# An FFT convolution with an MLP on one core: reordered loads and transform front, fixed PSUM places, and product PSUM in two pools

## The chip, the cores and the metric

The kernel runs on one core of a Trainium2 chip. The metric is the device time of one execution in microseconds. Besides the time there is a profile of one execution: a page of shares and groups of instructions, and a trace that can be asked for a chain of waits, a timeline, or busy times in stretches. PE is TensorE (matmul, with PEld for its weight loads), DVE is VectorE, ACT is ScalarE, POOL is GpSimd, SP is the engine that issues most of the DMAs.

## The reference

Cut to what matters (S = 2048, D = 512, Dff = 1376, all inputs bf16):

```python
def _A_ref(q, k, v, shift_k, ssm_k, ssm_D):
    k_shift = sum over t of k_pad[:, t:t + S, :] * shift_k[:, ks - 1 - t]     # 4 taps, causal
    kv = k_shift * v
    y = irfft(rfft(kv padded to 2S) * rfft(ssm_k padded to 2S))[:, :S, :]     # causal long convolution
    y = y + kv * ssm_D
    return q * y

x = A_q
h = x + _A_ref(_layernorm(x), A_k, A_v, A_shift_k, A_ssm_k, A_ssm_D)
out = h + relu(_layernorm(h) @ B_w1) @ B_w2
```

## The kernel before

The long convolution is a length-4096 transform written as matmuls in two stages over a 64 by 64 split, and only its odd frequencies are used. Everything is emitted in one order by hand (`manual_schedule`), so each engine works through its instructions in the order of the source, and waits only for the tiles it reads or overwrites. A pool of tiles of one tag hands out its buffers in rotation; a new tile waits until all readers of the one before it in its buffer are done, and a new pool waits for the pools that held its space.

The stages, in order of time:

1. **Loads and tables (0 to 9 us).** SP issues `sk` (the filter, 2 MB, L95) and then eight transposing DMAs, kT and vT for four chunks of 512 tokens (L111 to L114). ACT issues `wsh` (L97) and the two `draw` loads of ssm_D (L102), spread over 64 rows each. DVE makes integer phases (`tsn` L189, `tcs` L206), ACT turns them into sine and cosine tables (`table`, L184; `cc_part` makes one of four pieces of the cosine table). POOL makes the diagonal tap weights `wdiag` (L222), the first-stage tables `f1hi`/`f1lo`, the negated sines `c2n` (L229), the block-diagonal tables `f2hi`/`f2lo` (L234) and `dtab`, a copy of `draw` (L235).
2. **Row transposes (9 to 16).** `to_rows` (L246) makes eight PE transposes of 128x128 each into one PSUM tile `pst` and copies it to `kfl`, on DVE and ACT in turn; eight calls.
3. **Taps and first stage of the filter (16 to 41).** Eight groups: `taps(c, h)` (L303) makes two accumulations of four matmuls into the two banks of one tile `pkv`, and DVE multiplies each by v into `sk`'s space (L310); `stage1` (L252) makes 64 small matmuls, each with 32 rows, into two PSUM tiles of two banks, which are copied to `a1k` (L239 on ACT, L241 on DVE). With `pairs` it makes 32 matmuls with 64 rows and the tables f2hi/f2lo instead. Three `cc_part` tables go between the groups on ACT. The PE instructions of a group are 8 tap matmuls and 64 first-stage matmuls, with as many weight loads (the page counts both).
4. **Transposes of kv (41 to 45, L340) and second stage of the filter (45 to 60, `stage2`, L281 and L283)** into `kf`, with dtab added (L363).
5. **First stage of kv (60 to 71)**: eight `stage1` calls with pairs, copied to `a1x`, the first tile of each by ACT, the second by DVE.
6. **Product (71 to 102).** For each of 16 frequency pairs: `product` makes the second stage into `u0`, `u1`, multiplied by kf on DVE and POOL; two steps later `finish` combines the products by matmuls with plus or minus the identity into `psy0`, `psy1` (L408), and copies them back over kf (L239, L241). x (`load_x`, L419) and w1 (L430) are loaded meanwhile.
7. **First inverse stage (102 to 120, `inv1`, L528)**: 16 calls into `psi1` tiles, copied to `ax`. Between the calls stand the layer norm of x, the twiddles `ecore` and the centring of w1: `column_means(n)` (L504) makes the mean of a quarter of w1's columns by matmuls into a tile `pm`; `center` subtracts it, for n = 0 and 1 on DVE out of PSUM, for n = 2 and 3 on POOL after a DVE copy to `wm` (L555).
8. **Second inverse stage, gating, MLP (121 to 218)**: `inv2` (L592) into `psz` and `psz0`, `gate` (L574, L577) on DVE, then `mlp1` (L604) and `mlp2` (L621), with the later `inv2` calls between them.

[...] Stages 2 to 5 share one pool `psF` of four two-bank tiles with one tag: `pst`, `pkv`, `ps1`, `pst2` and `ps2k` all rotate through it. The product stage has `psP`, two buffers each of u0, u1, psy0 and psy1, a bank each. The inverse has `psI` (three two-bank tiles) and `psC` (two one-bank `pm` tiles), both pushed after psP is popped, so that their first tiles wait for all readers of psP.

Of the kernel before, what the change touches and what calls it, by code (L numbers as in the profile page):

```python
# [9 lines left out]
ALU = mybir.AluOpType  # L10
# [46 lines left out]
def kernel(  # L57
# [32 lines left out]
    kvp = pl.push("kvp", side="right")  # L90
    psum = pl.push("psF", bufs=4, space=PSUM)

# [6 lines left out]
    draw = consts.tile([P, DC, 64], BF16, name="draw")  # L99
    for dp in range(2):  # L100
        src = bass.AP(tensor=A_ssm_D.tensor, offset=A_ssm_D.offset + 64 * dp, ap=[[0, 64], [P, DC], [1, 64]])
        nc.scalar.dma_start(out=draw[64 * dp:64 * dp + 64, :, :], in_=src)  # L102
    vT = [vp.tile([P, DC, 512], BF16, name=f"vT{c}") for c in range(4)]
# [5 lines left out]
    for c in range(4):  # L109
        if c == 0:  # L110
            nc.sync.dma_start_transpose(out=kT[c][:, :, 16:CH + 16], in_=k_d[0:CH, :])  # L111
        else:
            nc.sync.dma_start_transpose(out=kT[c][:], in_=k_d[CH * c - 16:CH * c + CH, :])
        nc.sync.dma_start_transpose(out=vT[c][:], in_=v_d[CH * c:CH * c + CH, :])  # L114


# [62 lines left out]
    def wrap(t, M):  # L179
        nc.vector.tensor_single_scalar(out=t, in_=t, scalar=M - 1, op=ALU.bitwise_and)  # L180
# [24 lines left out]
    _sin(dsc[:], t3[:], 64)  # L205
    nc.vector.tensor_single_scalar(out=tcs[:], in_=tsn[:], scalar=2048.0, op=ALU.add)  # L206
    wrap(tcs[:], 8192)
    cc_parts = [(p, dp) for p in cc for dp in range(2)]

    def cc_part():  # L210
        p, dp = cc_parts.pop(0)
        table(p, tcs, dp)
# [12 lines left out]
    nc.gpsimd.tensor_tensor(out=f1f[:], in0=f1f[:], in1=f1hi[:, 0:64], op=ALU.subtract)  # L225
    nc.gpsimd.tensor_copy(out=f1lo[:, 0:64], in_=f1f[:])
    for a, b in ((0, 8), (8, 16), (16, 22), (22, 24), (24, 32)):
# [3 lines left out]
    for f, g in ((f1hi, f2hi), (f1lo, f2lo)):  # L231
        for rg in range(DC):
            rows = slice(32 * rg, 32 * rg + 32)
            nc.gpsimd.tensor_copy(out=g[rows, 64 * (rg % 2):64 * (rg % 2) + 64], in_=f[rows, :])  # L234
    nc.gpsimd.tensor_copy(out=dtab[:], in_=draw[:].rearrange("p r g -> p g r"))  # L235

    def copy(eng, o, i):
        if eng == "A":
            nc.scalar.copy(out=o, in_=i)  # L239
        else:  # L240
            nc.vector.tensor_copy(out=o, in_=i)  # L241

    def bank2(name):
        return psum.tile([P, 2, 512], F32, tag="ps", name=name)

    def to_rows(src, q, fl, eng):  # L246
        pst = psum.tile([P, 2, 8, P], BF16, tag="ps", name="pst")
        for i in range(8):
            nc.tensor.transpose(out=pst[:, 0, i, :], in_=src[:, :, :, 8 * q + i], identity=ident[:])  # L249
        copy(eng, fl[:, :, :, 8 * q:8 * q + 8], pst[:, 0, :, :].rearrange("p i (d g) -> p g d i", d=2))  # L250

    def stage1(fl, a_out, gb, engs, pairs=False):  # L252

        pss = [bank2("ps1") for _ in range(2)]
        n, tabs = (2, (f2hi, f2lo)) if pairs else (4, (f1hi, f1lo))
        K = P // n
        for gi in range(8):
            for f in range(2):
                for t in range(n):
                    rows = slice(K * t, K * t + K)  # L260
                    if pairs:
                        o = pss[t][:, gi // 4, 128 * (gi % 4):128 * (gi % 4) + 128]
                    else:
                        o = pss[t // 2][:, t % 2, 64 * gi:64 * gi + 64]
                    nc.tensor.matmul(out=o, lhsT=fl[rows, 8 * gb + gi, :, :].rearrange("p d n -> p (d n)"),  # L265
                                     rhs=tabs[f][rows, :], start=(f == 0), stop=(f == 1),
                                     tile_position=(K * t, 0), skip_group_check=True)
# [35 lines left out]
    def taps(c, h):  # L303
        ps = bank2("pkv")
        for i in range(2):
            for j in range(KS):
                nc.tensor.matmul(out=ps[:, i, :], lhsT=wdiag[:, 2 * h + i, j, :],  # L307
                                 rhs=kT[c][:, 2 * h + i, 16 - j:CH + 16 - j], start=(j == 0), stop=(j == KS - 1))
        for i in range(2):
            nc.vector.tensor_tensor(out=kvp2[:, :, 2 * h + i, 8 * c:8 * c + 8, :].rearrange("p m a e -> p a m e"),  # L310
                                    in0=ps[:, i, :].rearrange("p (a m e) -> p a m e", a=8, e=2),
                                    in1=vT[c][:, 2 * h + i, :].rearrange("p (a m e) -> p a m e", a=8, e=2),
                                    op=ALU.mult)
# [16 lines left out]
    nc.gpsimd.tensor_copy(out=k1o[:], in_=k1i[:])  # L330
    nc.gpsimd.memset(mhalf[:], -0.5)
    pl.pop("kvp")
    xfp = pl.push("xfp", side="right")
# [3 lines left out]
    for q in range(8):  # L337
        pst = psum.tile([P, 4, P], F32, tag="ps", name="pst2")
        for i in range(4):
# [28 lines left out]
    for gb in range(8):  # L368
        stage1(xfl, a1x, gb, "AD", pairs=True)
    pl.pop("psF")  # L370
# [14 lines left out]
    def product(kp):  # L385
# [3 lines left out]
        for s in range(2):  # L389
            u = psum.tile([P, 2, 256], F32, tag=f"u{s}", name=f"u{s}")  # L390
            stage2(u, a1x, kp, s)
# [11 lines left out]
    def finish(at):  # L403
        kp, (tr, ti) = pending.pop(0)
        for s, (a, b, m) in enumerate(((tr[:, 0], ti[:, 1], ineg), (tr[:, 1], ti[:, 0], ipos))):
            psy = psum.tile([P, 512], F32, tag=f"psy{s}", name=f"psy{s}")
            for m_, t_, first in ((ipos, a, True), (m, b, False)):
# [24 lines left out]
    load_x(2)  # L432
    load_x(3)
    while pending:
        finish(16)
    pl.pop("psP")
    pl.pop("prod")
# [14 lines left out]
    act_pool = {0: late, 1: late}  # L452
    psum = pl.push("psI", bufs=3, space=PSUM)
    psum1 = pl.push("psC", bufs=2, space=PSUM)

# [44 lines left out]

    FS = 344
    cen = {}

    def column_means(n):  # L504
        cen[n] = psum1.tile([P, 512], F32, tag="pm", name="pm")
        for c in range(DC):
            nc.tensor.matmul(out=cen[n][:, 0:FS], lhsT=ones[:], rhs=w1[:, c, n * FS:(n + 1) * FS],
                             start=(c == 0), stop=(c == DC - 1))

    def center(eng, n, mean):  # L510
# [3 lines left out]

    wm = late.tile([P, 2, FS], F32, name="wm")

    ec_turns(0)
    ln1_stats(0)
    ec_turns(1)
    column_means(0)  # L520
    column_means(1)

# [13 lines left out]
    for b in range(16):  # L536
# [73 lines left out]
    def mlp2(sc, hook=None):  # L610
        h1T = h1s[sc]
        for i in range(4):
# [18 lines left out]
            if hook is not None:  # L631
                hook(i)

    pl.pop("psC")
    pl.pop("psI")
    psz = pl.push("psZ", space=PSUM)
# [84 lines left out]
```

## Time and profile before

| | us |
|---|---|
| six runs, median | 219.46 |
| lowest and highest | 217.75, 220.78 |
| the profiled execution, in all | 220.12 |
| its span, first to last instruction | 218.2 |

Busy time of each engine, its share of the span and number of instructions, and the busy tenths of 40 equal slices (5.46 us each) with the granted TensorE clock in tenths:

```profile
PE 195.7 (90%) x2251; PEld 137.9 (63%) x2267; DVE 143.4 (66%) x236; ACT 115.7 (53%) x177; POOL 79.1 (36%) x120
...
PE   0389879899997999998999799999999999999991
...
PEclk9999979999999999999999999999999999999999
```

A digit of 9 is 90% or more. Before 9.3 us PE has no data; from then on it is nearly always busy, and the clock is full but for slice 5 (27.3 to 32.7 us). [...] A wait is shown at the instruction that had to wait, with what released it; "issue" stands for a wait that no semaphore in the profile explains.

### The profile page before, as it was taken

The page shows a single profiled execution, that of the slowest core. Times are in us where ns is not written, and L with a number is a line of the kernel's source. Part 1 is how long each engine was busy: PE and PEld are TensorE (multiplying, and loading weights), DVE is VectorE, ACT ScalarE, POOL GpSimd, SP SyncE. Part 2 cuts the span into 40 slices and gives each one's busy share as a digit, 9 for nine tenths or more (in the row PEclk, how much of TensorE's full clock was granted, in tenths as well). Part 3 has the DMA queues.
Part 4 walks back from the last instruction along what each step waited for, and adds up shares of the span by engine and source line. Part 5 has one row for each costly group of instructions (what it writes and reads, how often), then busy time and mean ns, then how long its engine had stood idle before and what let it go on. Part 6 is the DMA issues. An engine that isn't in the chain of part 4 may idle for free.

```text
span 218.2 us, 5459 instructions
## 1 busy us (share of the span) xinstructions
PE 195.7 (90%) x2251; PEld 137.9 (63%) x2267; DVE 143.4 (66%) x236; ACT 115.7 (53%) x177; POOL 79.1 (36%) x120
## 2 busy tenths in 40 slices
PE   0389879899997999998999799999999999999991
PEld 0385434699986899995999754655646644444451
DVE  7965746776689899998495993897395470243031
ACT  2977718765598588885897138401550046016400
POOL 3299992000001899997648702020202011002000
PEclk9999979999999999999999999999999999999999
DMA  5999950000000004836932789394453430010012
GB/s 197 299 195 219 152 122 3 5 2 3 0 5 3 0 3 112 223 119 178 196 72 37 226 159 171 61 195 88 94 96 65 101 79 3 24 49 24 0 45 56
DMA packets 49513, 20.08 MB, mean 92 GB/s; under 512 B 44400, under 2 KB 47952, under 8 KB 49488
## 3 DMA queue, kind: packets, MB, share of 16 engines
q1 hardware_dynamic: 46816, 18.18, 40.2%
q10 hardware_dynamic: 2672, 1.54, 2.7%
q8 instruction: 18, 0.29, 0.6%
q14 instruction: 7, 0.06, 0.1%
HBM read 7.08 MB, written 2.10 MB: 42 GB/s over the span
## 4 chain that ended last, share of the span: by engine, by line
PE 81%; DVE 9%; DMA 5%; issue 2%; SPq 1%; ACT 1%; DVEq 0%; ACTq 0%
PE ps1m L604 18%; PE ps2m L621 15%; PE pkv L307 7%; PE psi L528 7%; PE psy L408 7%; PE pz L592 5%; DVE a1x L241 4%; DMA sk<-in_A_ssm_k_dram 4%; PE ps2k L281 3%; PE ps2k L283 3%; PE u L281 3%; PE u L283 3%; PE ps L265 3%; PE pst L249 3%; PE pst L340 2%
## 5 line engine op out<-in xcount | busy, mean ns | idle before, releaser
L606 ACT ACTIVATE h1T<-ps1m 128x512 bf16<-128x512 f32 (+1 forms) x44 | 26.0, 596 | 55.4 <-PE ps1m L604 55.4
L621 PE MATMUL ps2m<-w,h1T 128*128 128x512 bf16 (+2 forms) x179 | 38.6, 366 | 0.6 <-issue 0.3
L604 PE MATMUL ps1m<-xT,w 128*128 128x512 bf16 (+1 forms) x176 | 38.8, 379 | 0.3 <-DVE xT L577 0.3
L624 DVE SCALAR_TENSOR_TENSOR o<-ps2m,rstd,xh 128x512 bf16<-128x512 f32 (+1 forms) x17 | 12.2, 719 | 31.2 <-PE ps2m L621 28.7
L604 PEld LDWEIGHTS <-w 128*128 128x128 bf16 (+1 forms) x176 | 17.5, 100 | 20.5 <-DVE xT L577 0.5
L621 PEld LDWEIGHTS <-h1T 128*128 128x128 bf16 (+1 forms) x187 | 17.9, 98 | 19.2
L398 POOL TENSOR_TENSOR t<-usb,kf 128x320 fp32r<-128x320 f32 x32 | 28.3, 956 | 2.0 <-ACT usb L394 1.7
L398 DVE TENSOR_TENSOR t<-u,kf 128x704 fp32r<-128x704 f32 x32 | 26.7, 886 | 3.0 <-ACT usb L394 3.0
L478 POOL TENSOR_SCALAR rstd<-mv 128x4 f32<-128x4 f32 x8 | 2.3, 283 | 67.4 <-DVE mv L476 67.4
L474 DVE BATCH_NORM_STATS2 st<-xh 128x6 f32<-128x512 bf16 x32 | 19.7, 677 | 0.0
L239 ACT CAST kf<-psy 128x512 fp32r<-128x512 f32 x30 | 17.5, 646 | 1.9 <-PE psy L408 0.3
L592 PEld LDWEIGHTS pz<-ecore,ax 32*128 32x128 f32 x512 | 15.0, 186 | 3.4 <-issue 1.7
L574 DVE TENSOR_TENSOR qT<-pz,qT 128x1024 bf16<-128x1024 f32 x8 | 9.8, 1222 | 10.8 <-PE pz L592 6.6
L239 ACT CAST a1k<-ps 128x1024 fp32r<-128x1024 f32 x12 | 12.3, 1065 | 8.6 <-PE ps L265 8.6
L592 PE MATMUL pz<-ecore,ax 32*128 32x128 f32 (+7 forms) x512 | 15.7, 273 | 1.1 <-ACT ax L239 1.1
L307 PE MATMUL pkv<-kT,wdiag 128*128 128x512 bf16 x56 | 15.9, 404 | 0.4
L408 PE MATMUL psy<-t,ipos 128*128 128x512 f32 x48 | 16.0, 393 | 0.0
L310 DVE TENSOR_TENSOR sk<-pkv,vT 128x512 bf16<-128x512 f32 x16 | 10.3, 687 | 8.3 <-PE pkv L307 8.3
L528 PE MATMUL psi<-dre,kf 128*128 128x256 f32 x64 | 15.7, 287 | 0.0
L249 PE MATMUL pst<-ident,sk 128*128 128x128 bf16 x64 | 6.6, 282 | 9.8 <-DMA sk<-in_A_ssm_k_dram 9.3
L528 PE MATMUL psi<-dim,kf 128*128 128x256 f32 x64 | 15.4, 282 | 0.0
L239 ACT CAST ax<-psi 128x1024 fp32r<-128x1024 f32 x13 | 12.4, 1016 | 4.6 <-DVE st L474 3.0
(116 smaller groups left out, 391.1 us busy)
## 6 DMA issues: line engine op xcount, KB each, us to landing
sk<-in_A_ssm_k_dram SPq DMA_DIRECT2D x1, 2048.0 KB, 8.5
xh<-in_A_q_dram SPq DMA_DIRECT2D x16, 128.0 KB, 3.1
out_dram<-o SPq DMA_DIRECT2D x60, 32.0 KB, 1.6
w<-in_B_w_dram SPq DMA_DIRECT2D x1, 1376.0 KB, 6.4
w<-in_B_w_dram ACTq DMA_DIRECT2D x1, 1280.0 KB, 6.4
xh<-xT SPq DMA_TRANSPOSE x8, 3.2
w<-in_B_w_dram ACTq DMA_DIRECT2D x1, 96.0 KB, 6.2
draw<-in_A_ssm_D_dram ACTq DMA_DIRECT2D x2, 32.0 KB, 8.5
```

The costliest lines, as they stand in the source:

```text
L239: nc.scalar.copy(out=o, in_=i)
L249: nc.tensor.transpose(out=pst[:, 0, i, :], in_=src[:, :, :, 8 * q + i], identity=ident[:])
L281: nc.tensor.matmul(out=ps[:, kk, :], lhsT=at_k1(w_re, k1), rhs=a_in[:, k1, :], start=True, stop=False, skip_group_check=True)
L307: nc.tensor.matmul(out=ps[:, i, :], lhsT=wdiag[:, 2 * h + i, j, :], rhs=kT[c][:, 2 * h + i, 16 - j:CH + 16 - j], start=(j == 0), stop=(j = ...
L398: eng.tensor_tensor(out=t[:, :, j, :], in0=in0.unsqueeze(1).to_broadcast([P, 2, n, 2]), in1=kfr[:, :, j, ks], op=ALU.mult)
L408: nc.tensor.matmul(out=psy[:], lhsT=m_[:], rhs=t_.rearrange("p j k -> p (j k)"), start=first, stop=not first)
L474: nc.vector.bn_stats(out=st[:, i, :], in_=src[:, i, :])
L528: nc.tensor.matmul(out=ps[:, i // 2, i % 2, :], lhsT=kf[:, c, 4 * m:4 * m + 4, :].rearrange("p r k -> p (r k)"), rhs=d[:].rearrange("p d a ...
L592: nc.tensor.matmul(out=pz[:, rg, 32 * jl:32 * (jl + w)], lhsT=ax[rows, 64 * rho + n2, :, :].rearrange("p d g -> p (d g)"), rhs=ecore[q][ro ...
L604: nc.tensor.matmul(out=ps1[:fsz, :].rearrange("p (i t) -> p i t", i=4), lhsT=w1[:, c, fc * P:fc * P + fsz], rhs=hT[sc][:, :, c, :], start= ...
L606: nc.scalar.activation(out=h1T[:fsz, fc, :], in_=ps1[:fsz, :], func=ACT.Relu)
L621: nc.tensor.matmul(out=ps2[:, 0:w], lhsT=h1T[:ksz, fc, i * P:(i + 1) * P], rhs=w2[:ksz, fc, ds], start=(fc == 0), stop=(fc == NFC - 1))
```

## The change

It has these parts:

- The two `draw` loads move from ACT's queue, where they were second and third, to SP's, behind the eight transposes. The copy to `dtab` moves on POOL from behind f2hi/f2lo to behind the constants made after the group loop.
- The f2hi/f2lo copies move on POOL ahead of the negated sines.
- The phases `tcs` are made in two halves (`cc_turns`): one on DVE behind the row transposes' copies, one behind the first group's products. No `cc_part` stands ahead of the row transposes; the four stand behind groups 0, 1, 3 and 5.
- PSUM of stages 2 to 5: three two-bank tiles of a tag each, handed out in turn by `place`, and a pool `psT` of two one-bank tiles for the taps (`tap_bank`), each of which takes one of the two accumulations. Of every five row-transpose tiles two use the tap banks. After the group loop psT is popped, and its space becomes a fourth two-bank place (`psX`).
- Group 2 of the filter's first stage uses 64-row matmuls (`pairs`).
- In the first stage of kv, the second tile of group 4 is copied in two halves, one on DVE and one on ACT.
- The product's PSUM is in two pools, psU (u0, u1) and psY (psy0, psy1). psU is popped before the last `finish` calls, and `pm` tiles (psC) and one two-bank place (psIa) take its space; `column_means(0)` and `(1)` stand directly behind the last `finish`. The inverse's other two places (psIb) take psY's space.
- `column_means(3)` and its centring move behind the last `inv1`.

The core of the diff:

```diff
-    psum = pl.push("psF", bufs=4, space=PSUM)
+    psum = pl.push("psF", space=PSUM)
+    psum_t = pl.push("psT", space=PSUM)
...
-        nc.scalar.dma_start(out=draw[64 * dp:64 * dp + 64, :, :], in_=src)
...
         nc.sync.dma_start_transpose(out=vT[c][:], in_=v_d[CH * c:CH * c + CH, :])
+    for dp in range(2):
+        src = bass.AP(tensor=A_ssm_D.tensor, offset=A_ssm_D.offset + 64 * dp, ap=[[0, 64], [P, DC], [1, 64]])
+        nc.sync.dma_start(out=draw[64 * dp:64 * dp + 64, :, :], in_=src)
...
-    nc.vector.tensor_single_scalar(out=tcs[:], in_=tsn[:], scalar=2048.0, op=ALU.add)
-    wrap(tcs[:], 8192)
+    def cc_turns(a):
+        part = tcs[:, a:a + 16, :]
+        nc.vector.tensor_single_scalar(out=part, in_=tsn[:, a:a + 16, :], scalar=2048.0, op=ALU.add)
+        wrap(part, 8192)
...
+    places = [psum] * 3
+    turn = [0]
+
+    def place(shape, dtype, name):
+        i = turn[0] % len(places)
+        turn[0] += 1
+        return places[i].tile(shape, dtype, tag=f"ps{i}", name=name)
+
     def bank2(name):
-        return psum.tile([P, 2, 512], F32, tag="ps", name=name)
+        return place([P, 2, 512], F32, name)
+
+    def tap_bank(i, shape, dtype, name):
+        return psum_t.tile(shape, dtype, tag=f"pk{i}", name=name)
 
     def to_rows(src, q, fl, eng):
-        pst = psum.tile([P, 2, 8, P], BF16, tag="ps", name="pst")
+        shape = [P, 8, P]
+        pst = tap_bank(q % 5 - 3, shape, BF16, "pst") if q % 5 > 2 else place(shape, BF16, "pst")
...
-            copy(engs[h], a_out[:, :, 32 * gb:32 * gb + 32].rearrange("p c (g r) -> p c g r", r=DC)[:, :, :, 2 * h:2 * h + 2],
-                 src)
+            dst = a_out[:, :, 32 * gb:32 * gb + 32].rearrange("p c (g r) -> p c g r", r=DC)[:, :, :, 2 * h:2 * h + 2]
+            for g, eng in enumerate(engs[h]):
+                n = 8 // len(engs[h])
+                copy(eng, dst[:, :, g * n:g * n + n], src[:, :, g * n:g * n + n])
...
-    cc_part()
     for q in range(8):
         to_rows(skv, q, kfl, "DADADADA"[q])
+    cc_turns(0)
...
-        ps = bank2("pkv")
+        pss = [tap_bank(i, [P, 512], F32, "pkv") for i in range(2)]
...
-        stage1(kfl, a1k, gb, ("AA", "AD")[gb % 2])
-        if gb in (0, 2, 4):
+        if gb == 0:
+            cc_turns(16)
+        stage1(kfl, a1k, gb, ("AA", "AD")[gb % 2], pairs=(gb == 2))
+        if gb in (0, 1, 3, 5):
             cc_part()
+    pl.pop("psT")
+    places.append(pl.push("psX", space=PSUM))
...
-        stage1(xfl, a1x, gb, "AD", pairs=True)
+        stage1(xfl, a1x, gb, ("A", "DA" if gb == 4 else "D"), pairs=True)
...
-    psum = pl.push("psP", bufs=2, space=PSUM)
+    psu = pl.push("psU", bufs=2, space=PSUM)
+    psy_ = pl.push("psY", bufs=2, side="right", space=PSUM)
...
+    pl.pop("psU")
+    psum1 = pl.push("psC", space=PSUM)
+    psum_a = pl.push("psIa", space=PSUM)
...
     while pending:
         finish(16)
-    pl.pop("psP")
+    column_means(0)
+    column_means(1)
+    pl.pop("psY")
+    places[:] = [psum_a] + [pl.push("psIb", side="right", space=PSUM)] * 2
+    turn[0] = 0
...
-    column_means(0)
-    column_means(1)
...
-        if b == 13:
-            column_means(3)
-        if b in (11, 14):
-            n = 2 + (b - 11) // 3
-            nc.vector.tensor_copy(out=wm[:, n - 2, :], in_=cen[n][:, 0:FS])
-            center(nc.gpsimd, n, wm[:, n - 2, :])
+        if b == 11:
+            off_center(2)
+    column_means(3)
+    off_center(3)
     ln1_stats(1)
```

More of the change, by code (lines that the diff above doesn't have):

```diff
@@ L99 @@
     draw = consts.tile([P, DC, 64], BF16, name="draw")
-    for dp in range(2):
-        src = bass.AP(tensor=A_ssm_D.tensor, offset=A_ssm_D.offset + 64 * dp, ap=[[0, 64], [P, DC], [1, 64]])
-        nc.scalar.dma_start(out=draw[64 * dp:64 * dp + 64, :, :], in_=src)
     vT = [vp.tile([P, DC, 512], BF16, name=f"vT{c}") for c in range(4)]
@@ L226 @@
     nc.gpsimd.tensor_copy(out=f1lo[:, 0:64], in_=f1f[:])
+    for f, g in ((f1hi, f2hi), (f1lo, f2lo)):
+        for rg in range(DC):
+            rows = slice(32 * rg, 32 * rg + 32)
+            nc.gpsimd.tensor_copy(out=g[rows, 64 * (rg % 2):64 * (rg % 2) + 64], in_=f[rows, :])
     for a, b in ((0, 8), (8, 16), (16, 22), (22, 24), (24, 32)):
@@ L230 @@
                                        op=ALU.mult)
[L231 to L235, printed above, removed]
     def copy(eng, o, i):
@@ L241, in copy @@
             nc.vector.tensor_copy(out=o, in_=i)
+    places = [psum] * 3
[4 more added lines that the diff above has]
+        return places[i].tile(shape, dtype, tag=f"ps{i}", name=name)
     def bank2(name):
-        return psum.tile([P, 2, 512], F32, tag="ps", name=name)
+        return place([P, 2, 512], F32, name)
+    def tap_bank(i, shape, dtype, name):
+        return psum_t.tile(shape, dtype, tag=f"pk{i}", name=name)
     def to_rows(src, q, fl, eng):
-        pst = psum.tile([P, 2, 8, P], BF16, tag="ps", name="pst")
+        shape = [P, 8, P]
+        pst = tap_bank(q % 5 - 3, shape, BF16, "pst") if q % 5 > 2 else place(shape, BF16, "pst")
         for i in range(8):
-            nc.tensor.transpose(out=pst[:, 0, i, :], in_=src[:, :, :, 8 * q + i], identity=ident[:])
-        copy(eng, fl[:, :, :, 8 * q:8 * q + 8], pst[:, 0, :, :].rearrange("p i (d g) -> p g d i", d=2))
+            nc.tensor.transpose(out=pst[:, i, :], in_=src[:, :, :, 8 * q + i], identity=ident[:])
+        copy(eng, fl[:, :, :, 8 * q:8 * q + 8], pst[:].rearrange("p i (d g) -> p g d i", d=2))
     def stage1(fl, a_out, gb, engs, pairs=False):
@@ L303, in taps @@
     def taps(c, h):
-        ps = bank2("pkv")
+        pss = [tap_bank(i, [P, 512], F32, "pkv") for i in range(2)]
         for i in range(2):
             for j in range(KS):
-                nc.tensor.matmul(out=ps[:, i, :], lhsT=wdiag[:, 2 * h + i, j, :],
+                nc.tensor.matmul(out=pss[i][:], lhsT=wdiag[:, 2 * h + i, j, :],
                                  rhs=kT[c][:, 2 * h + i, 16 - j:CH + 16 - j], start=(j == 0), stop=(j == KS - 1))
@@ L310, in taps @@
             nc.vector.tensor_tensor(out=kvp2[:, :, 2 * h + i, 8 * c:8 * c + 8, :].rearrange("p m a e -> p a m e"),
-                                    in0=ps[:, i, :].rearrange("p (a m e) -> p a m e", a=8, e=2),
+                                    in0=pss[i][:].rearrange("p (a m e) -> p a m e", a=8, e=2),
                                     in1=vT[c][:, 2 * h + i, :].rearrange("p (a m e) -> p a m e", a=8, e=2),
@@ L331 @@
     nc.gpsimd.memset(mhalf[:], -0.5)
+    nc.gpsimd.tensor_copy(out=dtab[:], in_=draw[:].rearrange("p r g -> p g r"))
     pl.pop("kvp")
@@ L337 @@
     for q in range(8):
-        pst = psum.tile([P, 4, P], F32, tag="ps", name="pst2")
+        pst = place([P, 4, P], F32, "pst2")
         for i in range(4):
@@ L368 @@
     for gb in range(8):
-        stage1(xfl, a1x, gb, "AD", pairs=True)
+        stage1(xfl, a1x, gb, ("A", "DA" if gb == 4 else "D"), pairs=True)
+    pl.pop("psX")
     pl.pop("psF")
@@ L389, in product @@
         for s in range(2):
-            u = psum.tile([P, 2, 256], F32, tag=f"u{s}", name=f"u{s}")
+            u = psu.tile([P, 2, 256], F32, tag=f"u{s}", name=f"u{s}")
             stage2(u, a1x, kp, s)
@@ L405, in finish @@
         for s, (a, b, m) in enumerate(((tr[:, 0], ti[:, 1], ineg), (tr[:, 1], ti[:, 0], ipos))):
-            psy = psum.tile([P, 512], F32, tag=f"psy{s}", name=f"psy{s}")
+            psy = psy_.tile([P, 512], F32, tag=f"psy{s}", name=f"psy{s}")
             for m_, t_, first in ((ipos, a, True), (m, b, False)):
@@ L433, with column_means @@
     load_x(3)
+    pl.pop("psU")
+    psum1 = pl.push("psC", space=PSUM)
+    psum_a = pl.push("psIa", space=PSUM)
+    FS = 344
+    cen = {}
+    def column_means(n):
+        cen[n] = psum1.tile([P, 512], F32, tag=f"pm{n % 2}", name="pm")
+        for c in range(DC):
+            nc.tensor.matmul(out=cen[n][:, 0:FS], lhsT=ones[:], rhs=w1[:, c, n * FS:(n + 1) * FS],
+                             start=(c == 0), stop=(c == DC - 1))
     while pending:
         finish(16)
-    pl.pop("psP")
+    column_means(0)
[3 more added lines that the diff above has]
+    turn[0] = 0
     pl.pop("prod")
@@ L452 @@
     act_pool = {0: late, 1: late}
-    psum = pl.push("psI", bufs=3, space=PSUM)
-    psum1 = pl.push("psC", bufs=2, space=PSUM)
     def ec_turns(q):
@@ L499, in ln1_norm @@
         rows_T(qT[q], qln[:])
[L501 to L508, printed above, removed]
     def center(eng, n, mean):
@@ L515, with off_center @@
     wm = late.tile([P, 2, FS], F32, name="wm")
+    def off_center(n):
+        nc.vector.tensor_copy(out=wm[:, n - 2, :], in_=cen[n][:, 0:FS])
+        center(nc.gpsimd, n, wm[:, n - 2, :])
     ec_turns(0)
@@ L632, in mlp2 @@
                 hook(i)
+    pl.pop("psIa")
     pl.pop("psC")
-    pl.pop("psI")
+    pl.pop("psIb")
     psz = pl.push("psZ", space=PSUM)
```

## The prediction

> **What bounds the kernel now.** I read the shares of busy time first, then the chain of waits in order of time, then stretches of it as windows. TensorE (PE) is busy 90% of the span and 81% of the chain, so a change pays only where PE stands still or runs slowly. From the chain (start us, us, what):
>
> ```profile
> 0.72 8.49 DMA sk<-in_A_ssm_k_dram
> 9.26 4.31 PE pst L249 x40
> 13.59 1.24 DVE kfl L241
> 14.87 1.58 PE pst L249 x16
> ...
> 26.43 2.31 issue
> 28.74 0.20 PE ps L265 x2
> 28.94 0.32 PE pkv L307
> 29.32 2.42 PE pkv L307 x6
> ...
> 39.68 1.30 DVE sk L310 x2
> ...
> 68.22 2.37 DVE a1x L241 x2
> ...
> 101.60 0.70 DVE kf L241
> 102.35 1.34 PE pm L507 x8
> ...
> 117.77 0.60 PE pm L507 x4
> 118.37 1.92 PE psi L528 x16
> 120.31 1.02 ACT ax L239
> 121.37 2.18 PE pz L592 x62
> ```
>
> Besides the load at the start, PE stands on this chain at six places: the row transposes (L249), an "issue" wait inside a first-stage group (L265), the end of the taps (L310), the copies of a1x, the last copies of kf before the column means, the last copy of ax before inv2. The change touches all six.
>
> The issue wait needs explaining, since no semaphore ends it and the groups before and after it use the same tiles. A smaller one (0.12 us at 23.24) lies in the middle of the group before. Counting PE's weight loads and matmuls from the start, the first gap comes after about 446, the second after about 701: 255 apart. The page has the row that fits:
>
> ```profile
> q8 instruction: 18, 0.29, 0.6%
> ```
>
> Eighteen packets of 16 KB. In the trace's packet records two of them run from 21.08 to 22.26 and from 26.39 to 27.56, and PE resumes 1.1 us after each. The third starts at 30.55, when the kT/vT transposes' packets have just ended (30.6). I take the gaps as PE waiting for its own program behind the transposes. If the fetch is asked for as PE enters the block before (18.3 and 23.36), it takes 5.1 and 5.4 us there. The second block is used up in 3.1 us, hence 2.31 us of waiting. What follows is in the windows (the figure after POOL is the granted clock):
>
> ```profile
> 26.40:28.70 2.30, 0.03 (x4) 0.00 (x0) 0.75 (x2) 1.70 (x2) 1.95 (x10) 1.00 1.24 104
> 29.90:33.30 3.40, 3.35 (x71) 1.53 (x71) 1.59 (x3) 0.56 (x1) 3.09 (x11) 0.53 0.18 41
> ```
>
> For 3.4 us after the gap the clock is half, and the tap group there takes 2.42 us for six matmuls against 1.46 in its neighbours. From 28.94 to 35.35 two groups take 6.41 us; undisturbed ones have a pitch of 2.45 us (18.79 to 21.24), so this costs 1.5 us.
>
> [...]
>
> **The change part by part.** Times are those of the profiled execution: span 218.2 us, 220.12 us in all. That is 0.66 above the median of the six runs, 219.46; I take the sum off the median.
>
> *Loads.* The two ssm_D loads leave the ACT queue and go behind the eight transposes on SP. Their 512 packets of 128 B run at 8.25 to 9.99, 13 ns each (0.4 us over 16 engines), and meet only the tail of sk (to 8.88). Gain 0 to 0.3; I take 0.1. On SP they issue after 28.9, and SP's next DMA is xh at 83.75, so nothing is held. The dtab copy (POOL, 0.62 us) moves behind the constants, to about 35; its reader is the first kf sum, about 42.
>
> *Row transposes.* 64 at 107.5 ns (4.31 us for 40) are 6.9 us; now they take 7.2 (9.26 to 16.45), with one wait for a kfl copy. Five PSUM places in place of four, a 1.28 us table that leaves ACT ahead of its first copy, and 2.45 us of integer work that leaves DVE there remove it: gain 0.3. The integer halves (about 1.23 us each) return on DVE behind the last kfl copy and behind the first products. Reckoning DVE: first half 16.3 to 17.5, products to 18.9, second half to 20.1, next products to 21.4, copy to 22.6. The next taps need their first bank at 18.3, 20.75 and 23.7, free at 18.2, 20.8 and 23.3. So nothing, or 0.1. ACT gets four tables in the loop after groups 0, 1, 3, 5; the place that group 2 wants is free about 22.65, PE is there at 22.6. Nothing again; bound 0 to 0.5.
>
> *The 64-row group.* Group 2 becomes 32 matmuls and 32 weight loads for 64 and 64. The 64-row row of the a1x stage is 1.04 us, the 32-row one 0.61: +0.43. But 64 instructions fewer move the next block boundary out of group 3 into group 4, behind its taps. PE's time on the second block grows from 3.1 to 5.3 us: rest of group 2 0.8, group 3 2.45, taps of group 4 1.84, a bit of its stage 0.2. Against a fetch of 5.4 this leaves 0.1. The block before keeps its window of 4.9 against 5.1, so I allow 0.3; the block after has 4.75 while the transposes end. Gone are 2.31+0.12 of waiting, less 0.4 that stays, and 1.5 of slow clock: gain 3.5. Bounds: 0 (the fetch is late elsewhere) to 3.9. The f2 tables of this group move ahead of c2n on POOL (8 copies, 2.1 us, done about 17.4, needed 22.6); c2n ends at 28.6 for use at 41.
>
> *End of the taps.* One-bank tiles let a product start after four matmuls, so PE's wait for DVE, 0.86, goes. What is late next: the first transpose after the loop takes place 22 mod 4, the tile of group 7's first half, whose ACT copy (1.09 us) starts as the group ends. Wait 1.2: loss 0.35 (bounds 0 to 0.5).
>
> *The divided copy at group 4 of a1x.* The copies are 1.11 on ACT and a 1.18 pitch on DVE, with four places. A step-by-step tally of this stage with these rows ends at 70.6, as traced. With the division DVE gains 0.6, but ACT holds group 4's second tile until 67.5 in place of 67.05, and group 6 waits for that tile. Tally: 71.0. Loss 0.4; bounds -0.3 to 0.5, since the DVE relief would count if ACT had room.
>
> *Column means 0 and 1.* They no longer wait for the last kf copies: w1 landed by 95.3 and psU's readers end at 100.3, before the last psy matmuls (101.5). Their 1.2 us fill the 0.84 wait; inv1 starts at about 102.7 for 103.41. Gain 0.7 (0 to 0.85).
>
> *Column mean 3* goes behind inv1, into the wait for ax's last copy (1.06). That takes 0.6 off PE before it. But the DVE copy of the mean (0.51) then waits for it, and behind it on DVE are four bn_stats and aggregates (2.8 us) and the first gate, which now starts at 123.64 as those end. They move back about 0.4 against inv1's end. Gain 0.2 (-0.3 to 0.6).
>
> Sum: loads -0.1, rows -0.3, fetch and clock -3.5, 64-row group +0.43, end of the taps +0.35, a1x +0.4, first means -0.7, last mean -0.2: -3.6. On the profiled execution that is 216.5; off the median, 219.46 - 3.6 is about **215.8 us**.
>
> **Rivals.**
>
> *The fetch is late all the same*, because it follows the DMA traffic and not the count, or half of the gap stays with its slow clock. For it: packet three waited until the transposes had ended. Against it: the two loaded fetches took nearly the same 5.1 and 5.4. With the whole 3.5 gone the sum is -0.1: 219.4; with half, 217.6. Chance 0.20 together.
>
> *One-bank taps serialise PE and DVE*: slower. If the next taps can start only when both products are read, PE waits from 0.61 (stage 1 behind the taps) to 1.34 us (both products, 18.1 to 19.5): 0.73 at each of seven groups, 5.1 us, and [...]one more spell of half clock, 1.5. That gives 215.8+6.6 = 222.4. It decides once DVE comes to a group's first product over 1.4 us after the taps end. Against it: the two banks are separate tiles, and my DVE reckoning keeps ahead by 0.1 at the tightest. Chance 0.08.
>
> *More than forecast*: the new waits at 37 and in a1x don't come (0.35+0.4), the divided copy gains 0.3 and the last mean its full 0.6: 215.8-1.5 = 214.3. Chance 0.08.
>
> The forecast itself has 0.64, own range 214.6 to 217.2.
>
> **How the numbers follow.** About 1% (2.2 us) is what a measurement of this kernel, whose runs spread from 217.75 to 220.78, tells from no change. Faster by over 1% (below 217.3): forecast, the better case, and little of the fetch rival: 0.72. Within 1%: the rest of the fetch rival: 0.19. Slower: 0.09, with accidents. The range 214.0 to 218.7 takes in the forecast, the better case and the half-kept stall.
>
> **What would show it.** No issue gap over 0.5 us and no half clock between 20 and 40; the block boundary in group 4. The transposes of L340 start at about 37.6, waiting for an ACT copy of a1k. The a1x stage lasts 0.4 longer. The pm matmuls follow psy without a gap; psi starts 0.7 sooner after the last psy. The first gate starts about 0.4 later against psi's end. A half clock spell in the front would make it wrong, as would waits of PE for L310.

## The result and the profile after

The changed kernel takes 219.92 us (median of 35 runs, 217.07 to 221.70) against 218.87 us for the kernel before (70 runs, 216.28 to 221.06): ratio 1.0049 [1.0028, 1.0071]. It was forecast 3.6 us faster and is about 1 us slower. The profiled execution took 218.84 us, its span 217.1.

From the page: busy times, the slices of PE and of the granted clock, the program's DMA queue, the chain by engine.

```profile
PE 195.6 (90%) x2220; PEld 137.7 (63%) x2235; DVE 143.6 (66%) x238; ACT 116.8 (54%) x178; POOL 79.6 (37%) x120
...
PE   0399897999996999999998599999999999999992
...
PEclk9999999999999999999999979999999999999999
...
q8 instruction: 17, 0.28, 0.5%
...
PE 79%; DVE 6%; DMA 5%; ACT 4%; issue 3%; SPq 0%; ACTq 0%
```

Slice 5 (27 to 32.6 us) has its 9 and its full clock back. Instead PE has a 5 in slice 22 (119.4 to 124.8) and the clock a 7 in slice 23. The gap has moved 94 us down the kernel. The program now comes in 17 packets instead of 18.

The chain of waits, first the front and then around inv2 (start us, us, what):

```profile
22.28 0.27 PE ps L280 x6
22.55 0.51 issue
23.07 0.90 PE ps L280 x26
...
35.61 0.69 PE ps L280 x64
36.30 1.11 ACT a1k L242
37.41 0.09 issue
37.50 3.88 PE pst L362 x32
```

```profile
115.28 0.61 PE pm L467 x4
115.89 0.02 issue
115.92 0.53 DVE wm L547
116.44 0.14 issue
116.58 4.06 PE pz L621 x126
120.64 2.31 issue
122.94 2.57 PE pz L621 x59
125.52 4.52 PE ps1m L633 x15
```

In the front 2.31+0.12 us of issue waits have become 0.51, and the transposes of kv start at 37.50 for 41.11 before. In inv2, where the kernel before ran through, there is an issue wait of 2.31, again with no semaphore behind it. The windows (start and end, length, busy us of PE, PEld, DVE, ACT, POOL, then granted clock, DMA share, GB/s) show the load beside it and what follows:

```profile
118.00:120.00 2.00, 2.00 (x83) 2.00 (x77) 2.00 (x7) 0.00 (x0) 1.92 (x3) 1.00 1.07 366
120.60:122.90 2.30, 0.04 (x2) 0.00 (x0) 2.27 (x4) 0.00 (x0) 0.10 (x1) 1.00 0.63 130
124.70:128.10 3.40, 3.40 (x20) 1.50 (x17) 3.38 (x11) 0.60 (x1) 0.00 (x0) 0.54 0.81 141
```

The DMA engines are full (share 1.07, 366 GB/s) just before the gap, and behind it the clock is half for 3.4 us: by the trace's own record of the clock from 124.45, 1.5 us after the gap, to 127.86 (the third window begins a little late and has 0.54). This is the front's pattern over again. What fills the engines is w2's load, on ACT's timeline:

```profile
115.32 0.40 ACTq L594 DMA_DIRECT2D w<-in_B_w_dram  x1
```

Checkpoints of the two profiled executions, in us:

```
                                  before    after   after - before
transposes of kv start             41.11    37.50       -3.61
last copy of a1x ends              70.58    66.80       -3.78
inv2 starts                       121.37   116.58       -4.79
mlp1 starts                       127.51   125.52       -1.99
end of span                       218.2    217.1        -1.1
```

So 4.8 us are gained up to inv2, more than forecast. 2.8 are lost within inv2, and about 1 more behind it, nearly all while the clock is half. The profile flatters the change by a further 2.3: before's profiled run was 1.25 above its median and after's 1.1 below. Its mean granted clock was 0.991; most other runs of the changed kernel had 0.982 to 0.988 and 219.0 to 221.7 us, and the one run with 1.000 took 217.07. So the granted clock varies from run to run, by up to 0.018.

### The profile page after: what moved, and what is told of

It is laid out like the page before. It is cut to its first block, busy times and chain, and to the rows that moved or that the text cites. A ratio compares the mean times of both kernels' runs of the same rounds, so it can differ in the third digit from the quotient of the medians.

```text
span 217.1 us, 5398 instructions
## 1 busy us (share of the span) xinstructions
PE 195.6 (90%) x2220; PEld 137.7 (63%) x2235; DVE 143.6 (66%) x238; ACT 116.8 (54%) x178; POOL 79.6 (37%) x120
## 4 chain that ended last, share of the span: by engine, by line
PE 79%; DVE 6%; DMA 5%; ACT 4%; issue 3%; SPq 0%; ACTq 0%
PE ps1m L633 18%; PE ps2m L650 17%; PE pz L621 7%; PE pkv L324 6%; PE psy L432 6%; PE ps L280 4%; DMA sk<-in_A_ssm_k_dram 4%; PE ps2k L300 3%; PE ps2k L298 3%; PE u L298 3%; PE u L300 3%; PE psi L559 3%; PE pst L264 3%; PE pst L362 2%; ACT a1x L242 2%
## 5 line engine op out<-in xcount | busy, mean ns | idle before, releaser
L633 PE MATMUL ps1m<-xT,w 128*128 128x512 bf16 (+1 forms) x176 | 40.0, 387 | 0.0
L621 PE MATMUL pz<-ecore,ax 32*128 32x128 f32 (+7 forms) x512 | 16.5, 277 | 3.0 <-issue 2.3
L621 PEld LDWEIGHTS pz<-ecore,ax 32*128 32x128 f32 x512 | 15.5, 188 | 5.7 <-issue 4.2
L324 PE MATMUL pkv<-kT,wdiag 128*128 128x512 bf16 x57 | 14.8, 380 | 0.6 <-DVE sk L327 0.2
```

The source lines that it names most:

```text
L324: nc.tensor.matmul(out=pss[i][:], lhsT=wdiag[:, 2 * h + i, j, :], rhs=kT[c][:, 2 * h + i, 16 - j:CH + 16 - j], start=(j == 0), stop=(j == ...
L621: nc.tensor.matmul(out=pz[:, rg, 32 * jl:32 * (jl + w)], lhsT=ax[rows, 64 * rho + n2, :, :].rearrange("p d g -> p (d g)"), rhs=ecore[q][ro ...
L633: nc.tensor.matmul(out=ps1[:fsz, :].rearrange("p (i t) -> p i t", i=4), lhsT=w1[:, c, fc * P:fc * P + fsz], rhs=hT[sc][:, :, c, :], start= ...
```

## The experiments

**The theory**: PE's program comes in packets of 16 KB, each a block of about 256 instructions: in the changed kernel's records the two issue waits come after about 446 and 3002 of PE's instructions, weight loads included, and the packets that end them are the first and the last of eleven, so 255.6 instructions go to a packet. A packet that is in time starts about a block ahead of its use: the four ahead of the late one start after 1732, 1995, 2213 and 2499 instructions, 5.03, 6.06, 6.91 and 8.03 blocks behind the first wait, for uses at 6, 7, 8 and 9. The late one starts at its use, after 3002. With the 64-row group 64 instructions fewer stand ahead of everything behind it, so every later block boundary has moved too. One now lies six instructions behind the start of inv2, whose instructions are short (256 in 3.9 us), just as w2's load (1.4 MB) fills the DMA engines; the block's packet is late and PE runs dry. **The rivals**: w2's issue stands in the way on ACT's queue; the loads of ssm_D; the new PSUM places; another price of the product's two pools.

**1. The boundary back in its old place.** Group 0 of kv's first stage goes back to 32 rows, which adds the 64 instructions again behind the front (two tables stay in memory longer for that).

```diff
-        stage1(xfl, a1x, gb, ("A", "DA" if gb == 4 else "D"), pairs=True)
+        stage1(xfl, a1x, gb, ("A", "DA" if gb == 4 else "D"), pairs=(gb > 0))
```

> The changed kernel, with group 0 of kv's first stage in the 32-row form (64 PE instructions more, so that the block boundaries of PE's program behind it stand where they stood before the change). Theory (the boundary that left the front came back in inv2, where its fetch queues behind the load of w2): no issue wait over 0.5 us in the front or in inv2, and 3 to 4 us less than the changed kernel's 219.9: about 216. Rival (inv2 is late through DVE: the moved column mean, the statistics and the gates): the wait in inv2 stays and the time is that of the changed kernel, within 0.7 us. Second rival (the loss is in the one-bank taps or the divided copy): likewise unchanged.

215.42 us, ratio to before 0.9782 [0.9734, 0.9831]. PE's waits (total, times, longest):

```profile
PE pkv L324 <- DVE sk L327: 1.7, 2, 0.9
...
PE pst L362 <- ACT a1k L242: 1.3, 1, 1.3
PE pz L621 <- DVE wm L547: 0.7, 1, 0.7
```

The issue wait of inv2 is gone. It isn't that the edit speeds anything up on the way: in this profile the last 48 matmuls of inv1 start at 110.89, 1.4 us later than in the changed kernel (109.52), and the span ends at 214.5, 2.6 earlier. The taps' waits for DVE reach 1.7 us here.

**2. w2 loaded later**: its two DMAs behind the first relu of mlp1.

> The changed kernel, with the two loads of w2 issued behind the first relu of mlp1(0) in place of before inv2; block boundaries unchanged. Theory: the fetch at the start of inv2 finds idle queues and takes about 3 us, so the 2.3 us wait and the half clock behind it go: about 216 to 216.5, unless w2 is then late for mlp2(0), which would show as a wait of L650 on DMA. Rival (DVE in inv2): unchanged, 219.9.

219.37 us, 1.0013 [0.9979, 1.0046]. The wait in inv2 went, as expected; the time did not. PE's longest wait for another engine after the start:

```profile
PE pz L623 <- DVE qT L605: 1.9, 1, 1.9
```

w2's packets now start at 125.6 to 131.9, in front of the transposing DMAs of the next chunk; qT lands at 135.6, PE waits, and a half-clock spell follows at 139.0. One collision was exchanged for another, so this run tells that w2 makes the wait, not what the wait costs.

**3. The 64-row group undone, and alone.** First the changed kernel without it, then the kernel before with it (and f2's copies moved ahead for it).

```diff
-        stage1(kfl, a1k, gb, ("AA", "AD")[gb % 2], pairs=(gb == 2))
+        stage1(kfl, a1k, gb, ("AA", "AD")[gb % 2])
```

> The changed kernel with group 2 of the filter's first stage back in the 32-row form. Theory: the wait of about 2 us returns to the front with its half clock, none in inv2; the time is 217.5 to 219, since the other parts gain about 1 us together. Rival (64-row group has nothing to do with inv2): the wait in inv2 stays, and the front's comes on top: 222 to 223.

> The kernel before with the 64-row group alone (and the f2 tables ahead of the negated sines on POOL). Theory: the front's wait goes (3.4 us earlier at 41 us) and one of 2 to 3 us comes in inv2: within 1 us of the kernel before. Rival: the front gain stays to the end, 215.5 to 216.5.

Without it: 217.36 us, 0.9865 [0.9819, 0.991], and the front's wait is back in its old place, without a half clock this time:

```profile
25.77 0.60 PE ps L280 x62
26.36 2.36 issue
28.73 0.20 PE ps L280 x2
```

Alone: 216.98 us, 0.9842 [0.9799, 0.9885]. The expectation of a 2 to 3 us wait failed, although the boundary stands at the same place in inv2:

```profile
117.11 4.06 PE pz L592 x126
121.17 0.28 issue
```

So the moved boundary is not enough. Something else in the change makes its fetch late.

**4. Which part?** Four runs take parts of the change away or add them: mean 3 back between the inv1 calls; before with the 64-row group and the late mean 3; ssm_D back on ACT; before with the 64-row group and ssm_D on SP.

> The changed kernel with column mean 3 and its centring back between the inv1 calls. Theory (the fetch at the start of inv2 loses a race: in the changed kernel PE enters the block 1.26 us after the load of w2 is issued, since it waits for the mean's copy; with the 64-row group alone it enters it 1.06 us after, and the fetch came through in 2.1 us in place of 4.3): the packet starts about 2 us after inv2 begins, the wait in inv2 is under 1 us, and the time is 216.5 to 217.5. Rival (the fetch is late here whatever the order; the 64-row group alone had luck): a wait over 2 us and the changed kernel's 219.9.

> The kernel before with two parts: the 64-row group, and column mean 3 behind the last inv1. Theory of the race: the wait of over 2 us in inv2 comes back, with half clock: 218.5 to 220. Rival (the late mean matters only through the other parts): as with the 64-row group alone or 0.2 less, about 217.

> The changed kernel with the two ssm_D loads back on ACT's queue, where they stood (the dtab copy stays late). The fetch at the start of inv2 took 4.3 to 4.8 us in three profiles of kernels with these loads on SP, and 2.1 to 2.7 in two with them on ACT, at the same distance from the load of w2, which is the next large load on ACT's queue. Theory (what ACT's queue carried before decides how long w2 holds the fetch up): the packet starts within 3 us of inv2's start, the wait in inv2 is under 1.2 us, the time about 216.5 to 217.5. Rival (something else of the front or of the PSUM pools does it): over 2 us and about 219.9.

> The kernel before with two parts: the 64-row group, and the ssm_D loads on SP behind the transposes. Theory: the fetch at the start of inv2 becomes late by over 4 us, the wait is over 2 us with half clock behind it, and the time goes from 217.0 to 219.5 to 221. Rival: as with the 64-row group alone, 216.5 to 217.5.

In that order: 221.76 us (1.0109 [1.0054, 1.0164]); 216.88 (0.989 [0.9839, 0.9941]); 219.82 (1.0078 [0.9991, 1.0166]); 216.19 (0.9918 [0.9851, 0.9986]). Neither the last mean nor ssm_D decides: the wait stays in the first (2.9) and third (2.7) and stays small in the second and the fourth (0.7 each). With mean 3 in its old place the changed kernel looks slower still (all four runs are above 221), though the intervals of the two ratios touch.

**5. The change cut in two.** Once all of its front without the two product pools and the moved means; once before with the 64-row group and those pools and means (none of the other front parts). Beside them another execution of the changed kernel, and one with w2 issued by SP.

> The changed kernel without its second half: one product pool, the column means where they were (the front with the 64-row group and the divided copy stays). Theory A (the parts around the product make the fetch at inv2 late): the packet starts within 3 us of inv2's start as with the 64-row group alone, about 216.5 to 217.5. Theory B (the reordered front does): over 4 us, wait over 2 us, 220 to 222 as with mean 3 put back.

> The kernel before with the 64-row group, the two product pools, the early means 0 and 1 and the late mean 3. Theory A: the fetch is late by over 4 us, 219 to 221. Theory B: within 3 us, about 216.

> The changed kernel as it is, one more profile: its mean granted clock was 0.983 in half of its runs, two spells of half clock, while the profile shows one. Theory: both spells are in and behind inv2; the fetch starts about 4 us after inv2 begins again. Rival: a second place loses clock, in the front (37, 66) or in the product.

> The changed kernel with the two loads of w2 issued on SP's queue at the same place in the order. Theory (PE's fetch waits for the load's packets, whichever queue carries them): no change, wait over 2 us, 219.9. Rival (ACT's queue is what holds the fetch): the packet starts within 2 us, about 216.5.

Front only: 216.93 us, 0.9915 [0.989, 0.9941]:

```profile
PE pz L620 <- issue: 0.6, 1, 0.6
```

Pools, means and 64-row group: 219.11, 1.0027 [0.9996, 1.0058]:

```profile
PE pz L597 <- issue: 2.5, 1, 2.5
```

So the late fetch comes with the two pools and the early means 0 and 1, which were not taken apart; the late mean alone does not bring it (experiment 4). The other execution of the changed kernel had a wait of 2.9 and again one half-clock spell. w2 on SP: 219.79, 0.9999 [0.9967, 1.0031], wait 3.2; so it is the load's traffic, not its place on ACT.

The packet records show what the late fetch waited for. For each profile whose block boundary and w2's load both lie at the start of inv2, in us: PE's first record of inv2 (a wait for a semaphore), its first weight load there, the first packet of w2, the start of the next block's packet, this start less the first record, the share of w2's 1376 packets that had started before it, and the total of half clock before 140 us.

```
kernel                   first   weights    w2     fetch   fetch-first  w2 ahead  half clock
changed                  116.47  116.55   116.39  120.64      4.17         91%      3.4
changed, again           116.72  116.80   116.63  121.38      4.66        100%      3.4
ssm_D on ACT             115.91  115.98   115.84  120.39      4.48         99%      6.8
w2 on SP                 116.73  116.80   116.66  121.52      4.79        100%      6.8
64 rows + pools          116.04  116.12   115.96  120.43      4.39         97%      6.8
mean 3 back              117.95  118.28   118.27  122.73      4.78         98%      6.8
64 rows alone            116.36  117.11   117.11  118.90      2.53         30%      0
64 rows, late mean 3     116.40  117.13   117.15  119.54      3.14         49%      0
64 rows, ssm_D on SP     115.79  116.54   116.54  118.95      3.16         45%      0
front only               116.90  117.65   117.68  119.92      3.01         38%      0
w2 issued later (7)      116.65  116.72   117.74  117.71      1.06          0%      0
```

In the first six kernels the packet starts only when 91 to 100% of w2's packets have: it waits for nearly the whole load, and lands after the block (3.9 us) is used up. In the next four less than half of the load is ahead of it, and it comes in 2.5 to 3.2 us, in time or nearly so (a packet takes 1.0 us). In the last none is ahead.

What decides between these is less clear. The semaphore record stands 0.75 us ahead of w2's first packet in the four kernels without the new pools, and 0.1 behind to 0.3 ahead in those with them. But the first weight loads stand level with that packet (within 0.03 us) in these four and in "mean 3 back" as well, where the fetch is late. That the fetch waits for the load is shown, since the wait goes when the load is moved (experiments 2 and 7). How much lead the fetch needs, and which instruction starts it, is not.

**6. Only the count.** The changed kernel with 16 matmuls of 64 columns into a spare bank, ahead of the transposes of kv. They compute nothing that is used and add 32 PE instructions.

```diff
+    idle = tap_bank(0, [P, 512], F32, "idle")
+    for _ in range(16):
+        nc.tensor.matmul(out=idle[:, 0:64], lhsT=ident[:], rhs=ident[:, 0:64], start=True, stop=True)
```

> The changed kernel with sixteen matmuls of 64 columns more (32 PE instructions, read by nobody) in the wait ahead of kv's transposes. Theory (only where the block boundary falls counts): the boundary comes 26 instructions ahead of inv2, its fetch is asked for before the load of w2 is issued and comes through at once, no wait in inv2, no half clock: 216 to 217 although PE does more. Rival: unchanged, 219.9 or 0.4 more.

214.85 us, 0.9818 [0.9751, 0.9885]: with added work the kernel is 1.8% faster than before, where the changed kernel is 0.5% slower. The packet now comes at 112.03, before w2's first (115.72). The clock is full, and PE's waits have no issue wait in inv2:

```profile
PE u L298 <- DVE a1x L244: 1.5, 1, 1.5
PE pz L624 <- DVE wm L550: 0.7, 1, 0.7
PE ps1m L636 <- DVE xT L609: 0.4, 1, 0.4
PE pst L365 <- issue: 0.3, 1, 0.3
```

Not all of the gain need be the fetch's: in this profile the added matmuls stand where PE waited for the a1k copy, and the transposes of kv start at 36.93, 0.57 us earlier than in the changed kernel.

**7. Only the race.** The instructions of PE stay as they are; w2's issue is held up by about a microsecond with a small write of DVE into w2's tile behind the last copy of a mean. For that, `ln1_stats(1)` on DVE moves from ahead of w2's loads to behind them.

```diff
-    ln1_stats(1)
...
+    nc.vector.memset(w2[:, :, 0:2], 0.0)
...
+    ln1_stats(1)
```

> The changed kernel with a small DVE write into w2's tile behind the last mean's copy, so that the two loads of w2 are issued about 1.2 us later, after PE has entered inv2; block boundaries as in the changed kernel. Theory (a race after all, counted from PE's first instruction of inv2: in the ten profiles the fetch is quick where that lies 0.75 us ahead of w2's first packet, and late where it lies 0.3 ahead to 0.1 behind): the first packet of w2 comes about 117.8, PE's first instruction 1 us earlier, the fetch starts within 3 us of it, the wait in inv2 is under 1 us, the time 216 to 217. Rival (not the order of the two requests): wait over 2 us, 219.9.

216.19 us, 0.9837 [0.978, 0.9895]. ACT issues w2 1.35 us later:

```profile
116.67 0.40 ACTq L594 DMA_DIRECT2D w<-in_B_w_dram  x1
```

The block's packet comes at 117.71, 1.06 us after inv2's first record in place of 4.17. There is no issue wait in inv2 and no half clock before the end. What is left in inv2 is the wait for DVE at its start, as long as in the changed kernel (0.7):

```profile
PE pz L622 <- DVE w L593: 0.7, 1, 0.7
```

Delaying one DMA's issue by 1.35 us takes the ratio from 1.005 to 0.984.

**8. What else was to be had.** Two kernels also copy the whole of each second a1x tile on DVE and shift the PSUM places by three, so that the transposes of kv take a place that is free: one on top of experiment 1, one on top of experiment 6.

```diff
+    turn[0] += 3
...
-        stage1(xfl, a1x, gb, ("A", "DA" if gb == 4 else "D"), pairs=True)
+        stage1(xfl, a1x, gb, "AD", pairs=(gb > 0))
```

> The changed kernel with the 32-row group 0 in kv's first stage (as in the realigned one), the second tiles of a1x all copied by DVE, and the places shifted by three behind the group loop, so that the first transposes of kv write a place whose reader is done. Theory: the realigned kernel's 215.4, less 0.3 to 0.4 in the a1x stage and 0.5 at the transposes: 214.6. Rival (the divided copy is worth its place): 215.4 or more.

> The changed kernel with the 32 PE instructions more ahead of kv's transposes, no divided copy and the places shifted by three: 214.85 of the shifted kernel less 0.3 in a1x and up to 0.5 at the transposes, about 214.2. Rival: the shift of places only moves the wait, 214.8.

214.88 us (0.9797 [0.9738, 0.9857]) and 214.86 us (0.9785 [0.9734, 0.9836]). In the first the wait at the transposes shrinks from 1.3 to 0.3:

```profile
PE pst L363 <- ACT a1k L242: 0.3, 1, 0.3
```

In its profile the second waits 1.6 us for the products of the taps, and its time is that of experiment 6:

```profile
PE pkv L324 <- DVE sk L327: 1.6, 2, 0.9
```

These two and those of experiments 1 and 6, all about 2% faster than before, are the best versions found; their intervals overlap.

## Why the prediction was wrong

**The step that failed is the 64-row group**: "64 instructions fewer move the next block boundary out of group 3 into group 4". That is right and was carried through the front alone. The same 64 are missing ahead of every later boundary. In the kernel before, the packet for inv2's block came at 115.61, with the DMA engines nearly idle (share 0.06 from 115.5 to 116.6) and some 8 us before it was needed, and the next at 125.87. After the change the boundary lies six instructions into inv2 (about 2745 PE instructions from the start), the next one 3.9 us on. "Bounds: 0 (the fetch is late elsewhere)" meant only that the gain could be lost; no later place was looked for. What the runs show in its place is a fetch that starts 4.2 us after inv2 and leaves PE standing for 2.31 us, with half clock behind it. Moving only the boundary takes the kernel from 219.92 to 214.85 us (experiment 6, with up to 0.6 of it from the earlier transposes), moving only w2's issue to 216.19 (experiment 7).

**The column means and pools** are the other half: they were costed by their waits (-0.7 and -0.2), but with them the fetch also loses the race against w2 that it wins, or nearly, without them. Experiment 3 shows that either half gains without the other: 0.9842 for the group alone, 0.9865 for the rest. Part of the second figure is that the half clock is missing behind its gap in the front (granted clock 0.998 to 1.0 in all four runs), which is not a gain of its parts by any term of the sum.

Point by point, by the terms of the sum:

- *Fetch and clock in the front*, -3.5: happened. There is one issue wait of 0.51 (forecast 0.4), no half clock before 120. With loads, rows, group and end of taps the forecast gave -3.1; the transposes start 3.61 earlier.
- *End of the taps*: right in kind and size. The transposes start at 37.50 (forecast 37.6) and wait for the ACT copy of a1k; the shift of places in experiment 8 takes about 1 us of that wait away.
- *One-bank taps*: no serialising. But "0.1 at the tightest" was too small: PE's waits for DVE's products come to 0.2 us in the changed kernel's profile and to 0.9 to 1.7 in eight of the thirteen profiles with this front.
- *The divided copy*: from the first DVE copy of the stage to the end of the last it is 9.77 in place of 9.46 us, +0.31 (forecast +0.4).
- *Means 0 and 1*: pm follows psy without a gap and from the end of the last psy to the first psi it is 0.9 us for 1.9. *Mean 3*: inv2 starts 1.0 further ahead than the end of a1x did (-4.79 for -3.78), against a forecast of -0.9 for both means.
- *The fetch rival* (chance 0.20) had the right kind of event, a fetch late all the same, but put it into the front and had no case slower than before. That the gain would be paid back with more behind the front was in no rival.
- *The reading of the packets*: in the trace the front's two late packets start at 20.84 and 26.15, 0.24 us before the times that the prediction gives, so PE went on 1.3 and 1.4 us after they ended and not 1.1. No term of the sum rests on it.
- *The base*: the median of six, 219.46, was 0.6 above that of 70 runs.

Without the late fetch the forecast's level is reached: 215.42, 214.85 and 216.19 us in experiments 1, 6 and 7, for 215.8.

That the fetch starts only when 91 to 100% of w2's packets have started was measured in six kernels (the table in experiment 5); which queue and packet held it up was not isolated.

**The half clock.** No experiment was made on why it follows some gaps and not others, but the traces narrow it. In the traces' records of the clock the spells behind the gaps of the kernel before and of the changed kernel last 3.413 us each. In each profile with a spell behind a gap and another at the very end, the two start a whole number of steps of 3.413 us apart (before: 29.67 and 217.40, 55 steps; changed: 124.45 and 216.61, 27), so each of these profiles can be cut into such steps. In the step ahead of the spell PE stood still for 2.36 us in the kernel before and for 1.91 in the changed kernel. In experiment 3's first kernel the gap falls across two steps, with 0.97 and 1.50 us, and no spell follows. Where the half clock lasts 6.8 us, PE stood still in the first half-clock step too, for 0.76 to 1.16 us. In the two kernels' profiles, from 12 us on and ahead of the last step, the most in any other full-clock step is 1.31 us (before) and 1.28 (changed), and no half clock follows. In these three profiles 1.50 us of standing still in a step was not followed by half clock and 1.91 was; where the limit lies, and whether the time of standing still alone sets it, they don't show.

**Open**: how the pools and the early means make the fetch late, and how much lead over the load it needs. Neither this nor the account of the half clock was tried by itself.

## What to carry to other kernels

Count PE's instructions, weight loads included. Mark off the packets of the program (255.6 instructions each here), and look where these marks fall against dense stretches of short matmuls and against large loads: an edit that changes the count moves every mark behind it (here 64 instructions fewer brought one to the start of inv2, and a wait of 2.31 us). Before a gain or loss is put down to an edit's own work, try the edit with the count made up again (a few matmuls that nobody reads), and move a large load by a microsecond.

## What was not expected of the hardware

- A program packet started 1.06 us after PE's first record of inv2 where no packet of a large load was ahead of it. Where a load of 1.4 MB started within 0.2 us of PE's first weight load there, it took 2.5 to 3.2 us in four kernels and 4.2 to 4.8 us in six; in these six nearly the whole load went first.
- A gap of 2.31 us was followed by 3.4 us of half clock that began 1.5 us after it, in a stretch where PE was fully busy; in four other executions, with gaps of 2.5 to 3.2 us, half clock began within the gap and lasted 6.8 us.
- 32 PE instructions of no use took the ratio to before from 1.005 to 0.982.
